# Attention decode backward on one core: where two more dK products stand relative to the softmax's reciprocal

## The chip, the cores and the metric

The kernel runs on one core of one Trainium2 chip. The metric is the device time of one execution in microseconds. Three executions of the kernel before took 634.61, 634.72 and 635.17 us; their median, 634.72 us, is the time before.

## The reference

There are 32 heads, each with one query row of 128 values and 8192 rows of K and of V, all in bf16. The reference returns the output and the three gradients of a softmax attention:

```
scores = einsum('bhqd,bhkd->bhqk', q, k) * 128 ** -0.5
p      = softmax(scores, axis=-1)
out    = einsum('bhqk,bhkd->bhqd', p, v)
# vjp with grad_out (the kernel's do):
dV = p outer do                 # 8192 x 128 per head
dp = V . do,  ds = p * (dp - sum(p * dp)) * scale
dK = ds outer q                 # 8192 x 128 per head
dq = ds . K
```

K and V are read once and dK and dV are written once: 134.23 MB each way by the profile. Each value read is used in very few operations.

## The kernel before, in words

The heads are worked in 16 pairs. In turn `t` of the main loop the pair `t` is "now" and the pair `o = t - 1` is "old". A pair's K is one SBUF tile of 128 partitions by 128 rows of 128 values, 4 MB; its V has the same shape. Three K tiles and two V tiles are used in rotation. The products dK and dV are written over K and V in place, and the stores read from these same tiles. That gives the cycle that every turn obeys: the tile is loaded, read by TensorE and VectorE, overwritten on VectorE by its gradient, stored, and, when the store has landed, loaded again for a later pair.

A pair passes through these steps, with the engine that does each:

- `k_block(t, c)`, eight of them: VectorE transposes an eighth of K (L197), TensorE multiplies it with q into the bank `s_ps` (L205).
- `s_back`, `s_top`, `s_exp`, `s_sum`: VectorE takes the scores back and their maximum (L212, L217, L219), TensorE turns the maximum (L220), VectorE makes the bias `nbias` (L227), ScalarE makes the exponentials `e` (L230), TensorE sums them over the partitions (L235, into `m_ps`).
- `p_of`: VectorE takes the reciprocal `rinv` of that sum (L246) and a scaled copy `p_s` (L251). ScalarE makes `p_rep` from `e` and `rinv` (L248) and puts it into the windows `win_p` (L241).
- `contract(t, "p")`: TensorE multiplies V with `win_p` (L341, `acc_p`), for the output.
- `v_bank`, `v_copy` and `v_scores`: TensorE transposes V (L269, `T_ps`), sixteen banks of four 128x128 pieces, ScalarE copies each bank out (L275, `XV_sb`), TensorE multiplies with `do` (L286, `dp_ps`). Three PSUM buffers serve the banks.
- `v_back`, `pd_sum`, `ds_of`, `contract(t, "ds")`: VectorE takes dp back (L312, `dpT`), and the softmax gradient `ds` is made and contracted with K.
- `outer(t, "p", r)` and `outer(o, "ds", r)`, eight of each: VectorE overwrites block `r` of V with dV, or of K with dK (both L363). A block of V can be overwritten only after `contract(t, "p")` and the transposes of that block have read it. `dk(a, b)` runs the dK products `a` to `b - 1` of the old pair, and issues the store (L373) that a finished part allows.

All instructions stand on each engine in the order in which the Python code lists them: no scheduler moves them, and each engine works through its own list in order. All loads and large stores are issued from one queue, SyncE's, in list order too.

There are two kinds of turn. In turns 3 to 14 (`wide(t)`, "with V blocks") half of V is transposed by VectorE instead of TensorE. Turns 0, 1, 2 and 15 do without V blocks, and all sixteen banks of V go over TensorE; turn 16 has only the dK products of the last pair and the small results. In turn 0 there is no old pair, so `dk` issues nothing.

In turns 1, 2 and 15 VectorE's order in the kernel before is: dK products 0 to 2, the scores' way back and `nbias`, dK product 3, the reciprocal, `p_s`, dK products 4 to 7, dV products 0 and 1, `v_back`, dV product 2, `ds`, and the other dV products. The dK store follows product 7 (in turn 15 there are two half stores, after products 3 and 7); the dV store follows dV product 7 (in turn 15 there are four, after every second product).

Of the kernel before, what the change touches and what calls it, by code (L numbers as in the profile page):

```python
# [15 lines left out]
NB = 8  # L16
# [11 lines left out]
def kernel(  # L28
# [54 lines left out]
    def load_k(t, parts=1):  # L83
        load(k, Kt, t, parts)
# [124 lines left out]
    def s_back(t):  # L209
        x = st[t]  # L210
        x["sT"] = backs.tile([P, BN, QD], F32, tag="back", name="sT")
        nc.vector.transpose(x["sT"][:].rearrange("p n r -> p (n r)"), x.pop("s")[:])  # L212

    def s_top(t):
        x = st[t]
        mx = small.tile([P, 1], F32, tag="mx")
        nc.vector.reduce_max(mx[:], x["sT"][:, :, 0:NB], axis=AX.XY)  # L217
        top = small.tile([P, 1], F32, tag="top")
        nc.vector.tensor_scalar_mul(top[:], mx[:], scale)  # L219
        nc.tensor.transpose(x["m"][:, 128:256], top[:].to_broadcast([P, P]), ident_f[:])  # L220

    def s_exp(t):
        x = st[t]
        nbias = small.tile([P, 1], F32, tag="nbias")
        for s in range(2):
            a, b = s * HF, (s + 1) * HF
            nc.vector.tensor_reduce(nbias[a:b], x["m"][a:b, 128 + a:128 + b], axis=AX.X, op=ALU.max, negate=True)  # L227
        e = x["e"] = single.tile([P, NT], F32, tag="e", name="e")
        rs = small.tile([P, 1], F32, tag="rs")
        nc.scalar.activation(e[:].rearrange("p (c n) -> p n c", c=NB), x["sT"][:, :, 0:NB], ACT.Exp, bias=nbias[:],  # L230
                             scale=scale, accum_out=rs[:])
        return rs
# [20 lines left out]
    def wide(t):  # L253
        return 3 <= t < HP - 1

    def v_bank(t, m):
        x = st[t]
        z, i = divmod(m, NM // TB)
        if t == 0:
            if i == 0:  # L260
                x["XV", z] = k_in[2][:].rearrange("p n d -> p (n d)").bitcast(F32).rearrange(
                    "p (z m s) -> p z m s", z=NZ, s=P)[:, z]
        elif i == 0:
            x["XV", z] = xvpool.tile([P, NM, P], F32, tag="XV", name="XV_sb")[:]
        T_ps = psT.tile([P, TB, P], F32, tag="T", name="T_ps")
        words = Vt[t][:].rearrange("p n d -> p (n d)").bitcast(F32)
        for j in range(TB):
            at = (i * TB + j) * NZ + z
            nc.tensor.transpose(T_ps[:, j, :], words[:, at * P:(at + 1) * P], ident_f[:])  # L269
        x["T", m] = T_ps  # L270

    def v_copy(t, m):
        x = st[t]
        z, i = divmod(m, NM // TB)
        nc.scalar.copy(x["XV", z][:, i * TB:(i + 1) * TB, :], x.pop(("T", m))[:])  # L275
# [14 lines left out]
    def v_block(t, r):  # L290

        X = xkpool.tile([P, NM, NW, QD], F32, tag="XK", name="XV_blk")
        nc.vector.transpose(X[:], Vt[t][:].rearrange("p n d -> p (n d)").bitcast(F32).rearrange(  # L293
            "p (m r w j) -> p m r w j", r=SL, w=NW, j=QD)[:, :, SL // 2 + r])
        st[t]["XW", r] = X
# [63 lines left out]
    def outer(t, which, r):  # L359
        x = st[t]  # L360
        X, row = (Kt[t], 0) if which == "ds" else (Vt[t], 1)
        a, b = r * BN, (r + 1) * BN
        nc.vector.tensor_tensor(  # L363
            X[:, a:b, :].rearrange("p n (a b) -> p n a b", b=R),
            x[which][:, a:b, :].unsqueeze(2).to_broadcast([P, BN, D // R, R]),
            x["qd"][:, row, :].rearrange("p (a b) -> p a b", b=R).unsqueeze(1).to_broadcast([P, BN, D // R, R]),
            op=ALU.mult)

    def store(t, which, parts=1, last=None):
        X, dst = (Kt[t], out_2) if which == "ds" else (Vt[t], out_3)  # L370
        L = NT // parts
        for c in (range(parts) if last is None else (last,)):
            nc.sync.dma_start(rows_of(dst, t, c * L, (c + 1) * L), X[:, c * L:(c + 1) * L, :])  # L373
# [15 lines left out]
    def v_part(t, m):  # L389
        v_bank(t, m)  # L390
        v_copy(t, m)
# [19 lines left out]
    for t in range(HP + 1):  # L411
        o = t - 1
        now, old = t < HP, t > 0
        parts = 4 if o == HP - 1 else 2 if o == HP - 2 else 1

        def dk(a, b):
            for r in range(a, b if old else a):
                outer(o, "ds", r)
                if (r + 1) % (NB // parts) == 0:
                    store(o, "ds", parts, r * parts // NB)  # L420

        blocks = now and wide(t)

        if blocks:

            dk(0, 5)
            s_back(t)
            s_top(t)
            for m in range(3):
                v_bank(t, m)  # L430
            v_block(t, 0)
            rs = s_exp(t)
            for m in range(3):
                v_copy(t, m)
            v_block(t, 1)
            v_part(t, 3)
            s_sum(t, rs)
            v_scores(t, 0)
            v_wide(t, 0)
            dk(5, 6)  # L440
            p_of(t)
            v_part(t, 4)
            v_part(t, 5)
            v_block(t, 2)
            v_wide(t, 1)
            v_part(t, 6)
            v_part(t, 7)
            v_block(t, 3)
            contract(t, "p")
            v_scores(t, 1)  # L450
            v_wide(t, 2)
            v_wide(t, 3)
            weights_do(t + 1)
            if wide(t + 1):
                weights_wide(t + 1)
        else:
            dk(0, 3)
            if now:
                if old:
                    v_part(t, 3)  # L460
                    v_part(t, 4)
                s_back(t)
                s_top(t)
                if old:
                    v_scores(t, 0)
                    v_part(t, 5)
                    v_part(t, 6)
                rs = s_exp(t)
                if old:
                    for m in (7, 8, 9):  # L470
                        v_bank(t, m)
                s_sum(t, rs)
                if old:
                    v_copy(t, 7)
                    v_copy(t, 8)
            dk(3, 4)
            if now:
                p_of(t)
                if old:
                    v_copy(t, 9)  # L480
                    v_scores(t, 1)
                    v_part(t, 10)
                    v_part(t, 11)
                contract(t, "p")
                if old:
                    v_part(t, 12)
                    v_part(t, 13)
                    v_scores(t, 2)
                    v_part(t, 14)
                    v_part(t, 15)  # L490
                    v_scores(t, 3)
                if t + 1 < HP:
                    if old:
                        weights_do(t + 1)
                    if wide(t + 1):
                        weights_wide(t + 1)
        if not now:
            dk(4, NB - 1)
            results()
            dk(NB - 1, NB)  # L500
            break
        dk(6 if blocks else 4, NB)
        fine = t == 0 or t == HP - 1
        outer(t, "p", 0)
        outer(t, "p", 1)
        if fine:
            store(t, "p", 4, 0)
        v_back(t)
        pd_sum(t)
        if t % ST == 0 and old:  # L510
            gather(o, "ds")
        outer(t, "p", 2)
        ds_of(t)
        contract(t, "ds")
        if t % ST == ST - 1:
            gather(t, "p")
        if t + 1 < HP:
            prepare(t + 1)
        else:
            gather(t, "ds")  # L520
        for r in range(3, NB):
            outer(t, "p", r)
            if fine and r % 2:
                store(t, "p", 4, r // 2)
            if t + 1 < HP and t != 1 and r >= HALF - 1:
                k_block(t + 1, r - HALF + 1)
        if not fine:
            store(t, "p")
        if t == 1:
            for c in range(HALF + 1):  # L530
                k_block(t + 1, c)
        if t + 1 < HP:
            for c in range(HALF + 1, NB):
                k_block(t + 1, c)
                if not wide(t + 1):
                    v_part(t + 1, c - HALF - 1)
            if t + 2 < HP:
                weights_q(t + 2)
        if 0 < t and t + 2 < HP:
            load_k(t + 2)  # L540
        if t + 2 < HP:
            load_v(t + 2, 4 if t == 0 else 1)
# [32 lines left out]
```

## Time and profile before

| what | value |
|---|---|
| median of three executions | 634.72 us (634.61 to 635.17) |
| the profiled execution's own time | 635.36 us |
| span in its profile, first to last instruction | 633.6 us |
| VectorE (DVE) busy | 558.9 us, 88% |
| TensorE (PE) busy | 428.7 us, 68% |
| ScalarE (ACT) busy | 158.0 us, 25% |
| the large DMA queue (q1) | 268.47 MB, 99.2% of 16 engines' span |
| DMA over the span | 424 GB/s |

The profiled execution took 1.76 us more than its span; this lies around the first and the last instruction. It is 0.64 us above the median, so a sum made on the span is taken to the median by its difference alone. "Busy" is the time of an engine's instructions, and a share of the span. In the timeline a row holds the start, the duration, the engine, the line of the kernel, the operation, what it writes and reads, and how many instructions are merged; in brackets stands how long the engine was idle ahead of the row, and what released it.

### The profile page before, as it was taken

To read this page: it belongs to the slowest core of one execution; us is meant where nothing else is said; L and a number is where in the kernel's file an instruction comes from. 1 tells how busy PE (TensorE), PEld (TensorE's weight loads), DVE (VectorE), ACT (ScalarE), POOL (GpSimd) and SP (SyncE) were. 2 spreads that over 40 slices of the span, in tenths; PEclk is the share of its full clock that TensorE was granted. 3 is DMA by queue.
4 is the path that set the end of the run, shared out by engine and by line. 5 is a ranking of instruction groups with operands and counts; after the bars stand their busy time and mean duration, and the time that the engine had idled before them with its cause. 6 is when DMAs were issued, how large, how long until landed. Compare 5 with 4: busy or idle time off the path is not lost.

```text
span 633.6 us, 7259 instructions
## 1 busy us (share of the span) xinstructions
PE 428.7 (68%) x2876; PEld 231.2 (36%) x2876; DVE 558.9 (88%) x662; ACT 158.0 (25%) x407; POOL 9.5 (1%) x27
## 2 busy tenths in 40 slices
PE   6767777766685765847766676765768658576860
PEld 5225335242341523315342332523425233152630
DVE  3788997999979899998998989899898899989793
ACT  6013416031230412204031130311303113040520
POOL 2000000000000000000000000000000000000000
PEclk9879888879789777798878798687986878887865
DMA  8999999999999999999999999999999999999997
GB/s 355 440 428 398 438 418 415 425 430 409 432 433 431 435 431 431 435 432 431 429 431 430 432 431 430 430 432 438 436 426 434 431 434 427 432 430 429 426 414 325
DMA packets 12177, 268.92 MB, mean 424 GB/s; under 512 B 1520, under 2 KB 1520, under 8 KB 1520
## 3 DMA queue, kind: packets, MB, share of 16 engines
q1 hardware_dynamic: 12096, 268.47, 99.2%
q8 instruction: 22, 0.36, 0.2%
q14 instruction: 11, 0.09, 0.0%
q10 hardware_dynamic: 48, 0.01, 0.0%
HBM read 134.23 MB, written 134.23 MB: 424 GB/s over the span
## 4 chain that ended last, share of the span: by engine, by line
DVE 38%; DMA 27%; PE 22%; issue 9%; ACT 2%; DVEq 0%; SPq 0%; ACTq 0%
DVE XK_sb L197 15%; DMA K<-in_k_dram 14%; DMA out_dram<-K 13%; DVE K L363 11%; PE T_ps L269 10%; DVE V L363 6%; PE dp_ps L303 5%; PE acc_p L341 3%; PE dp_ps L286 2%; ACT XV_sb L275 1%; DVE sT L212 1%; DVE dpT L312 1%; PE m_ps L220 1%; DMA V<-in_v_dram 1%; DVE ds_rep L331 1%
## 5 line engine op out<-in xcount | busy, mean ns | idle before, releaser
L205 PE MATMUL s_ps<-XK_sb,q_win 128*128 128x512 bf16 x512 | 148.6, 431 | 50.5 <-DVE XK_sb L197 48.3
L197 DVE STREAM_TRANSPOSE XK_sb<-K 128x1024 f32<-128x1024 f32 x128 | 152.2, 1221 | 3.5 <-DMA K<-in_k_dram 3.3
L363 DVE TENSOR_TENSOR V<-p_rep,qd 128x2048 bf16<-128x2048 bf16 x128 | 152.0, 1203 | 3.2 <-DMA K<-in_k_dram 2.0
L363 DVE TENSOR_TENSOR K<-ds_rep,qd 128x2048 bf16<-128x2048 bf16 x128 | 147.8, 1207 | 0.1
L269 PE MATMUL T_ps<-ident_f,V 128*128 128x128 f32 x640 | 108.1, 333 | 0.3 <-DMA V<-in_v_dram 0.2
L205 PEld LDWEIGHTS <-q_win 128*128 128x128 bf16 x512 | 53.4, 106 | 138.6 <-issue 102.7
L269 PEld LDWEIGHTS T_ps<-ident_f,V 128*128 128x128 f32 x640 | 97.5, 176 | 14.5 <-ACT XV_sb L275 1.6
L275 ACT COPY XV_sb<-T_ps 128x512 f32<-128x512 f32 x144 | 79.0, 586 | 78.7 <-PE T_ps L269 78.3
L293 DVE STREAM_TRANSPOSE XV_blk<-V 128x1024 f32<-128x1024 f32 x48 | 59.6, 1241 | 9.1 <-PE dp_ps L303 8.7
L341 PE MATMUL acc_ds<-K,win_ds 128*32 128x512 bf16 x512 | 47.8, 540 | 27.8 <-ACT win_ds L241 27.8
L220 PE MATMUL m_ps<-ident_f,top 128*128 128x128 f32 x16 | 6.2, 389 | 72.6 <-DVE top L219 72.6
L303 PE MATMUL dp_ps<-XV_blk,do_wide 128*128 128x512 bf16 x192 | 51.2, 399 | 0.0
L182 ACT COPY q_win<-q_blk 128x16 bf16<-128x16 bf16 x16 | 4.2, 260 | 156.7 <-PE s_ps L205 156.2
L341 PE MATMUL acc_p<-V,win_p 128*32 128x512 bf16 x512 | 32.1, 394 | 2.6 <-ACT win_p L241 2.4
L341 PEld LDWEIGHTS <-win_ds 128*32 128x32 bf16 x512 | 15.9, 122 | 48.1 <-ACT win_ds L241 27.2
L220 PEld LDWEIGHTS m_ps<-ident_f,top 128*128 128x128 f32 x16 | 2.6, 161 | 79.4 <-issue 71.4
L286 PE MATMUL dp_ps<-XV_sb,do_win 128*32 128x512 bf16 x288 | 24.3, 413 | 8.1 <-ACT XV_sb L275 8.1
L230 ACT ACTIVATE e<-sT,nbias 128x128 f32<-128x128 f32 x16 | 8.2, 515 | 80.8 <-DVE nbias L227 80.8
L303 PEld LDWEIGHTS <-do_wide 128*128 128x128 bf16 x192 | 17.3, 100 | 28.3 <-issue 14.3
L312 DVE STREAM_TRANSPOSE dpT<-dp_ps 128x512 f32<-128x512 f32 x16 | 11.5, 717 | 13.9 <-PE dp_ps L303 13.0
L341 PEld LDWEIGHTS <-win_p 128*32 128x32 bf16 x512 | 13.0, 99 | 16.3 <-issue 6.7
L321 PE MATMUL m_ps<-pd,same 128*128 128x1 f32 x32 | 6.1, 260 | 18.8 <-DVE m_ps L315 18.8
(68 smaller groups left out, 203.4 us busy)
## 6 DMA issues: line engine op xcount, KB each, us to landing
K<-in_k_dram SPq DMA_DIRECT2D x15, 4096.0 KB, 19.3
V<-in_v_dram SPq DMA_DIRECT2D x14, 4096.0 KB, 19.3
out_dram<-K SPq DMA_DIRECT2D x14, 4096.0 KB, 26.3
out_dram<-V SPq DMA_DIRECT2D x14, 4096.0 KB, 18.4
V<-in_v_dram SPq DMA_DIRECT2D x8, 1024.0 KB, 9.6
out_dram<-V SPq DMA_DIRECT2D x8, 1024.0 KB, 12.8
K<-in_k_dram SPq DMA_DIRECT2D x4, 1024.0 KB, 16.3
out_dram<-K SPq DMA_DIRECT2D x2, 2048.0 KB, 11.9
```

The source lines that it names most:

```text
L197: nc.vector.transpose(X[:], Kt[t][:, c * BN:(c + 1) * BN, :].rearrange("p n d -> p (n d)").bitcast(F32).rearrange("p (n w j) -> p n w j", ...
L205: nc.tensor.matmul(x["s"][:], lhsT=q_win[:, 2 * w + e2, SL - 1 - c:SL - 1 - c + P], rhs=cols[:, w, e2], start=(c == 0 and w == 0 and e2 == 0),
L220: nc.tensor.transpose(x["m"][:, 128:256], top[:].to_broadcast([P, P]), ident_f[:])
L230: nc.scalar.activation(e[:].rearrange("p (c n) -> p n c", c=NB), x["sT"][:, :, 0:NB], ACT.Exp, bias=nbias[:], scale=scale, accum_out=rs[:])
L269: nc.tensor.transpose(T_ps[:, j, :], words[:, at * P:(at + 1) * P], ident_f[:])
L275: nc.scalar.copy(x["XV", z][:, i * TB:(i + 1) * TB, :], x.pop(("T", m))[:])
L286: nc.tensor.matmul(x["dp"][b * QD:(b + 1) * QD, :], lhsT=do_win[:, b // 2, e2, at:at + QD], rhs=cols[:, e2, :, b * QD:(b + 1) * QD], start ...
L293: nc.vector.transpose(X[:], Vt[t][:].rearrange("p n d -> p (n d)").bitcast(F32).rearrange("p (m r w j) -> p m r w j", r=SL, w=NW, j=QD)[:, ...
L303: nc.tensor.matmul(st[t]["dp"][:], lhsT=do_wide[:, 2 * w + e2, at:at + P], rhs=cols[:, w, e2], start=False, stop=(r == SL // 2 - 1 and w = ...
L312: nc.vector.transpose(dpT[:].rearrange("p m r -> p (m r)"), x.pop("dp")[:])
L341: nc.tensor.matmul(acc[which][b * QD:(b + 1) * QD, :], lhsT=win[which][:, g, at:at + QD], rhs=X[:, 4 * g:4 * g + 4, :].rearrange("p n d -> ...
L363: nc.vector.tensor_tensor(X[:, a:b, :].rearrange("p n (a b) -> p n a b", b=R), x[which][:, a:b, :].unsqueeze(2).to_broadcast([P, BN, D // ...
```

## The change

In the turns without V blocks that have an old pair and a new one (1, 2 and 15), dK products 4 and 5 of the old pair are put ahead of `p_of`, so that six dK products stand ahead of the reciprocal instead of four. The loop that issues the rest then begins at 6 in these turns, as it did in the turns with V blocks. In turn 16 the two edits of `dk` ranges give the same products in the same order.

```
@@ -473,7 +473,7 @@
                 if old:
                     v_copy(t, 7)
                     v_copy(t, 8)
-            dk(3, 4)
+            dk(3, 6)
             if now:
                 p_of(t)
                 if old:
@@ -495,11 +495,11 @@
                     if wide(t + 1):
                         weights_wide(t + 1)
         if not now:
-            dk(4, NB - 1)
+            dk(6, NB - 1)
             results()
             dk(NB - 1, NB)
             break
-        dk(6 if blocks else 4, NB)
+        dk(6, NB)
         fine = t == 0 or t == HP - 1
         outer(t, "p", 0)
         outer(t, "p", 1)
```

The lists of ScalarE, TensorE, GpSimd and SyncE are the same in both kernels. On VectorE the reciprocal and `p_s` stand two products later in three places, and nothing else differs.

More of the change, by code (lines that the diff above doesn't have):

```diff
@@ L475 @@
                     v_copy(t, 8)
-            dk(3, 4)
+            dk(3, 6)
             if now:
@@ L497 @@
         if not now:
-            dk(4, NB - 1)
+            dk(6, NB - 1)
             results()
@@ L501 @@
             break
-        dk(6 if blocks else 4, NB)
+        dk(6, NB)
         fine = t == 0 or t == HP - 1
```

## Prediction

> **What bounds the kernel now.** I read the page first. VectorE is busy for 88% of the span and leads the chain of waits with 38%, so a VectorE stall looks like money. The DMA rows say otherwise:
>
> ```profile
> DMA  8999999999999999999999999999999999999997
> q1 hardware_dynamic: 12096, 268.47, 99.2%
> ```
>
> The first row is the mean busy share of the 16 DMA engines in 40 slices; only the ends are below 9. The second is the one large queue: 268.47 MB, with packets in flight for 99.2% of the 16 engines' span. Busy need not mean bound, so I looked at the order of landing in the stretch that the change touches (turn 1 runs from about 54 to 89 us). SyncE's timeline gives the issues:
>
> ```profile
> 68.95 0.34 SPq L373 DMA_DIRECT2D out_dram<-K  x1
> 80.30 0.34 SPq L373 DMA_DIRECT2D out_dram<-V  x1
> 84.58 0.34 SPq L81 DMA_DIRECT2D K<-in_k_dram  x1
> ```
>
> and the DMA view, in a window around each of these, gives size and time to landing (last column, us):
>
> ```profile
> out_dram<-K SPq DMA_DIRECT2D x1, 4096.0 KB, 15.6
> out_dram<-V SPq DMA_DIRECT2D x1, 4096.0 KB, 13.9
> K<-in_k_dram SPq DMA_DIRECT2D x1, 4096.0 KB, 19.4
> ```
>
> Issue plus time to landing: the dK store lands at 84.55, the dV store at 94.2, the K load at 104.0. They land in order of issue, 9.65 and 9.8 us apart, while each has been queued for longer than that. So the queue works in order and one 4 MB transfer takes 9.7 us of it; what a transfer needs beyond 9.7 us is time that it stood behind others. I call that its cover: 15.6 - 9.7 = 5.9 us for the dK store, 4.2 us for the dV store, 9.7 us for the K load. A transfer issued earlier only waits longer; one issued later costs nothing until its cover is used up. In turn 2 it is the same: dK store 20.0 us to landing, cover 10.3; dV store 13.8, cover 4.1. In turn 15 the two half dK stores take 13.5 and 10.4 us against 4.85 of their own, the 1 MB dV stores 8.7 against 2.4, and the very last dK store 9.1 against 2.4. The whole run is 64 such 4 MB transfers: 64 x 9.7 = 621 us of 633.6. The DMA queue is the bound.
>
> **What is stalled where.** VectorE's timeline of turn 1, with the idle time before a row in brackets:
>
> ```profile
> 59.88 1.23 DVE L363 TENSOR_TENSOR K<-ds_rep,qd 128x2048 bf16<-128x2048 bf16 x1
> 63.82 0.17 DVE L246 RECIPROCAL rinv<-m_ps 128x1 f32<-128x1 f32 x1 [2.72 <-PE m_ps L235]
> 64.30 4.62 DVE L363 TENSOR_TENSOR K<-ds_rep,qd 128x2048 bf16<-128x2048 bf16 x4
> 68.84 2.35 DVE L363 TENSOR_TENSOR V<-p_rep,qd 128x2048 bf16<-128x2048 bf16 x2
> 71.49 0.72 DVE L312 STREAM_TRANSPOSE dpT<-dp_ps 128x512 f32<-128x512 f32 x1 [0.30 <-PE dp_ps L286]
> ```
>
> VectorE stands idle for 2.72 us ahead of the reciprocal, in front of work (four dK products) that was ready. It is idle again, for only 0.30 us, ahead of `dpT`. That second bracket names TensorE, whose own timeline is:
>
> ```profile
> 59.76 3.80 PE L269 MATMUL T_ps<-ident_f,V 128*128 128x128 f32 x20
> 63.36 0.42 PE L235 MATMUL m_ps<-rs,same 128*128 128x1 f32 x2
> 65.60 1.91 PE L341 MATMUL acc_p<-V,win_p 128*32 128x512 bf16 x32
> 67.44 1.09 PE L269 MATMUL T_ps<-ident_f,V 128*128 128x128 f32 x8
> 70.83 0.62 PE L286 MATMUL dp_ps<-XV_sb,do_win 128*32 128x512 bf16 x8 [0.72 <-ACT XV_sb L275]
> ```
>
> The sum (L235) stands behind twenty transposes of V; the last dp matmuls end at 71.45, just before `dpT`. Turns 2 and 15 are alike: 2.83 us of idle time ahead of the reciprocal in both, and 0.31 and 0.36 us ahead of `dpT`.
>
> **The change, step by step.** (1) Two products go into the hole. Four in a row took 4.62 us, 1.155 each, so 2.31 us. Product 3 starts at 59.88; three of them end near 59.88 + 3.45 = 63.33 (3.45 is what three in a row took at 54.32). The reciprocal was released at 63.8, so it starts when it did, with 0.45 us to spare; in turn 15, 593.28 + 3.45 = 596.73 against 597.34, 0.6 to spare. Cost nothing; the cover is TensorE's twenty transposes. Behind the reciprocal stand `p_s` on VectorE, and `p_rep` with three bank copies queued after it on ScalarE; TensorE's `acc_p` and everything down to the last dp matmul wait for these. None of them moves. That the products themselves grow beside TensorE's transposes I put at nothing: the three at 54.32 ran beside such transposes and bank copies.
>
> (2) After `p_s` two dK products are left instead of four, so they end at 64.30 + 2.31 = 66.6 instead of 68.9, and the dK store is issued 2.3 us sooner. SyncE's list is unchanged and nothing stands between. The store lands at 84.55 as before, because the queue in front of it is what it waits for: its time to landing grows to 17.9. The K load that waits for this landing stays at 84.58. Gain nothing.
>
> (3) dV products 0 and 1 come next on VectorE, but they overwrite V, which TensorE still reads: `acc_p` until 67.5, and the transposes of these blocks in the first half of the row at 67.44, to about 68.0 (68.5 if the wait covers the whole row). So VectorE waits about 1.4 us here, where it did not wait before, and the two products end at about 70.4 (70.9).
>
> (4) `dpT` waits for TensorE at 71.45 as before; its idle time goes from 0.30 to about 1.1 us (0.6). The 2.31 us taken from the hole come back as 1.4 + 0.8 ahead of these two rows. From `dpT` on, VectorE stands where it stood, and so do the dV store and the next pair's scores.
>
> Sum per turn: 0; three turns: 0. The span stays 633.6 and the profiled time 635.36; from the median, 634.72 + 0 = 634.7 us.
>
> What the trace doesn't settle are two small ends. Below: the earlier second half store in turn 15 (602.46 to about 600.2) might fill a thin place, since between 600 and 604 the 16 engines' share dips to 0.62 to 0.85 for parts of a microsecond; the missing share there adds up to under 0.5 us, so at most 0.5 us is won. Above: if the two products overran the release by up to 0.5 us per turn, `dpT` and the dV store would be 0.5 us late against a cover of 4.1 us, so again nothing. I take 0 and keep -0.5 for the range.
>
> **Rivals.** *Faster: the DMA queue follows VectorE.* If DMA were only busy and not the bound, and if `dpT` could come earlier too, the 3 x 2.31 = 6.9 us would be won: 634.7 - 6.9 = 627.8 us. For it: VectorE's 88% and its lead in the chain. Against it: steps 2 to 4, two independent reasons, and the landings 9.65 to 9.8 us apart. It needs `dpT` in the profile after to start 2 us earlier. 0.08. The Trainium skill, Perfetto Trace Analysis, "Identifying the Most-Contended Engine", speaks for it: occupancy is called misleading for the 16 DMA engines, and bytes moved should be judged instead. Here the two agree by what the rows show, 424 GB/s over the span and the even landings; by the 435 GB/s ceiling that DMA: Bandwidth & Descriptors gives under "Specifications" the bytes would need 617 us, an estimate that leaves some 16 us of room.
>
> *Slower: TensorE's chain is granted less clock.* The granted clock is uneven in exactly this stretch (columns: window, its length, busy time of PE, PEld, DVE, ACT, POOL, then the clock, the DMA share and GB/s):
>
> ```profile
> 62.00:64.00 2.00, 2.00 (x14) 1.83 (x16) 0.17 (x1) 1.08 (x4) 0.00 (x0) 0.51 1.02 430
> 64.00:66.00 2.00, 1.86 (x24) 1.12 (x20) 1.91 (x3) 1.85 (x5) 0.00 (x0) 1.00 1.00 422
> ```
>
> If VectorE's new work beside the transposes went with a longer half-rate stretch, the chain from the sum to `dpT` (about 7.6 us of TensorE rows between 63.36 and 71.45) would stretch with it. A half-rate stretch like that from 60.5 to 64 costs some 1.7 us. The point from which it decides is the dV store's cover, 4.1 to 4.2 us: one or two stretches more cost nothing, three cost 5.1 - 4.2 = 0.9 us per turn. In turns 1 and 2 that is 1.8 us, 636.5 us; with the whole chain at half rate 7.6 - 4.2 = 3.4 us per turn, 641.5. Against it: TensorE's list and its idle gaps are untouched. 0.09. The Trainium skill, TensorE: Matmul & The Clock Gate, Part 1, makes the gate follow TensorE's own recent activity in a free-running window, so that its phase may vary between runs; by it the change has no handle on the clock, and the trace agrees in so far as the 0.51 follows TensorE's own wait at 57 to 59 us.
>
> *The change does nothing as written.* VectorE's list does differ in the three places, so that is excluded; what remains is that it does so to no effect, which is the forecast.
>
> **How the numbers follow.** Forecast, no change: 0.83. Faster by the rival: 0.08. Slower: 0.09. A measurement of this kernel can tell about 0.2% (1.27 us) from no change, and the forecast with its ends lies inside that, so the chances of faster, same and slower are 0.08, 0.83 and 0.09. The range is the forecast's own, which with 0.83 holds what is asked: the lowest execution less the 0.5 us end and 0.2 of scatter, 634.61 - 0.7 = 633.9, to the profiled execution's time plus 0.2, 635.6.
>
> **What would show it.** In the profile after, for turn 1: idle ahead of the reciprocal 0.4 to 0.5 us and its start still 63.8; the dK store issued near 66.6 with a time to landing of 17.9; new idle time of about 1.4 us ahead of dV product 0, about 1 us ahead of `dpT`, and `dpT` still at 71.5; dV store at 80.3 and K load at 84.6. The forecast is wrong if `dpT` starts over 0.5 us earlier and the landings move with it, or if landings in a row come more than 10 us apart because the dV store was issued after its cover had run out.

## The result, and the profile after

The changed kernel takes 636.76 us (median of 13, 635.51 to 637.04) against 635.11 us for the kernel before on the same chip (median of 13, 634.61 to 635.69). The ratio is 1.0022, with a 95% interval of 1.0015 to 1.0030: the kernel became slower by about 1.4 us by the ratio (the medians lie 1.65 us apart). Its 13 times form two groups: three lie at 635.5 to 635.9 and ten at 636.35 to 637.04. The profile after is of the shortest one, 635.51 us with a span of 633.7, beside 633.6 before. So the first profile shows where the two products went, but hardly the loss.

VectorE's timeline of turn 1 after, to be laid beside the rows of before:

```profile
59.90 3.50 DVE L363 TENSOR_TENSOR K<-ds_rep,qd 128x2048 bf16<-128x2048 bf16 x3
63.90 0.17 DVE L246 RECIPROCAL rinv<-m_ps 128x1 f32<-128x1 f32 x1 [0.51 <-PE m_ps L235]
64.38 2.35 DVE L363 TENSOR_TENSOR K<-ds_rep,qd 128x2048 bf16<-128x2048 bf16 x2
68.06 2.36 DVE L363 TENSOR_TENSOR V<-p_rep,qd 128x2048 bf16<-128x2048 bf16 x2 [1.33 <-ACT XV_sb L275]
71.61 0.72 DVE L312 STREAM_TRANSPOSE dpT<-dp_ps 128x512 f32<-128x512 f32 x1 [1.18 <-PE dp_ps L286]
```

This is the forecast, row for row: 0.51 us are left of the hole, the dV products wait 1.33 us, and `dpT` starts at 71.61 (71.49 before). The bracket of the dV products names ScalarE's copies, but the last of those in front of it ended at 67.1; the eight transposes of V on TensorE that began at 67.53 took 1.09 us, and their first half ends near 68.1, so the wait fits them, as step 3 said. SyncE's timeline and, in the second fence, the DMA view around each issue (last column: us to landing) after:

```profile
66.76 0.34 SPq L373 DMA_DIRECT2D out_dram<-K  x1
80.42 0.34 SPq L373 DMA_DIRECT2D out_dram<-V  x1
84.52 0.34 SPq L81 DMA_DIRECT2D K<-in_k_dram  x1
```

```profile
out_dram<-K SPq DMA_DIRECT2D x1, 4096.0 KB, 17.7
out_dram<-V SPq DMA_DIRECT2D x1, 4096.0 KB, 13.7
```

The dK store is issued 2.2 us sooner and still lands at 84.5; the dV store lands at 94.1. The queue's row is the same to the last digit as before:

```profile
q1 hardware_dynamic: 12096, 268.47, 99.2%
```

What belongs to this execution alone is on TensorE:

```profile
59.78 3.86 PE L269 MATMUL T_ps<-ident_f,V 128*128 128x128 f32 x20
63.44 0.43 PE L235 MATMUL m_ps<-rs,same 128*128 128x1 f32 x2
```

Twenty transposes in 3.86 us, as in the profile before (3.80). The granted clock in 60 to 64 us was 0.63 and 0.52. This is not how most of the traces of this case look: in 11 of 14 these twenty transposes of turn 1 take 2.5 us.

### The profile page after: what moved, and what is told of

It is laid out like the page before. It is cut to its first block, busy times and chain, and to the rows that moved or that the text cites. A ratio compares the mean times of both kernels' runs of the same rounds, so it can differ in the third digit from the quotient of the medians.

```text
span 633.7 us, 7259 instructions
## 1 busy us (share of the span) xinstructions
PE 427.7 (67%) x2876; PEld 229.6 (36%) x2876; DVE 559.3 (88%) x662; ACT 157.7 (25%) x407; POOL 9.5 (1%) x27
## 3 DMA queue, kind: packets, MB, share of 16 engines
HBM read 134.23 MB, written 134.23 MB: 424 GB/s over the span
## 4 chain that ended last, share of the span: by engine, by line
DVE 36%; DMA 31%; PE 19%; issue 9%; ACT 3%; DVEq 0%; SPq 0%; ACTq 0%
DMA out_dram<-K 18%; DVE XK_sb L197 15%; DMA K<-in_k_dram 12%; DVE K L363 11%; PE T_ps L269 10%; DVE V L363 5%; PE dp_ps L303 4%; PE acc_p L341 2%; PE dp_ps L286 2%; ACT XV_sb L275 1%; DVE sT L212 1%; DVE dpT L312 1%; DMA V<-in_v_dram 1%; PE m_ps L220 1%; ACT K L275 1%
## 5 line engine op out<-in xcount | busy, mean ns | idle before, releaser
L205 PE MATMUL s_ps<-XK_sb,q_win 128*128 128x512 bf16 x512 | 150.9, 433 | 52.1 <-DVE XK_sb L197 49.1
L269 PE MATMUL T_ps<-ident_f,V 128*128 128x128 f32 x640 | 106.2, 329 | 0.7 <-DMA V<-in_v_dram 0.4
L269 PEld LDWEIGHTS T_ps<-ident_f,V 128*128 128x128 f32 x640 | 95.8, 173 | 14.8 <-issue 1.9
L303 PEld LDWEIGHTS <-do_wide 128*128 128x128 bf16 x192 | 17.2, 100 | 27.8 <-issue 13.6
```

Of the source, the lines that this page charges most:

```text
L205: nc.tensor.matmul(x["s"][:], lhsT=q_win[:, 2 * w + e2, SL - 1 - c:SL - 1 - c + P], rhs=cols[:, w, e2], start=(c == 0 and w == 0 and e2 == 0),
L303: nc.tensor.matmul(st[t]["dp"][:], lhsT=do_wide[:, 2 * w + e2, at:at + P], rhs=cols[:, w, e2], start=False, stop=(r == SL // 2 - 1 and w = ...
```

## Experiments

All were timed in five rounds beside the kernel before on the same chip. Each has one profiled execution, which need not be a median one.

### Which turns, and is the loss real

**Six products ahead in turns 1 and 2 only** (the edit is to the kernel before).

```
-            dk(3, 4)
+            dk(3, 6 if t in (1, 2) else 4)
...
-        dk(6 if blocks else 4, NB)
+        dk(6 if blocks or t in (1, 2) else 4, NB)
```

> The change in turns 1 and 2 alone. Theory 'early': the loss comes from the first turns, where the two dK stores enter the DMA queue 2.2 us sooner; then this kernel is 1.0 to 1.8 us slower than before (ratio 1.0016 to 1.0028). Theory 'tail': the loss comes from turn 15, where the last stores are issued; then this kernel is within 0.4 us of before. Theory 'chance' (nothing real, the executions of both kernels only scatter): within 0.4 us, as are all four of this set.

Measured: 636.40 us (11 runs, 635.79 to 636.97) against 635.24; ratio 1.0017 (1.0008 to 1.0026).

**Six products ahead in turn 15 only** (`t == HP - 1` in the place of `t in (1, 2)`).

> The change in turn 15 alone. 'Tail': 1.0 to 1.8 us slower than before. 'Early': within 0.4 us. 'Chance': within 0.4 us. If both parts are slower by about half each, neither theory holds and the loss is a sum.

Measured: 635.13 us (11 runs, 634.79 to 635.49), ratio 0.9999 (0.9990 to 1.0008). Turn 15 costs nothing; the loss is that of turns 1 and 2. (In this trace the products overran the hole of turn 15 too: VectorE was not idle ahead of its reciprocal, which started at 597.61 us, 0.9 us after the sum.)

**The changed kernel again, and the kernel before against itself.**

> The changed kernel once more. 'Early' and 'tail': ratio 1.0015 to 1.003 as in the first comparison, most executions near 637.0 and a few near 635.6. 'Chance': ratio near 1.000. In its profile, if this execution is a long one, the extra 1.4 us should show as landings more than 9.7 us apart at one place: before 130 us by 'early', after 595 us by 'tail'.

> The kernel before, unchanged, as a measure of what the comparison itself can tell: ratio 1.000 within 0.0008 by every theory but 'chance', which expects it to scatter as the changed kernel does (634.6 to 637.0).

Measured: 636.67 us, ratio 1.0021 (1.0012 to 1.0030), and 635.40 us, ratio 1.0001 (0.9992 to 1.0010). The loss repeats, and a kernel against itself shows none. The profiled execution of the repeat took 637.13 us (span 635.3), so this is a trace of the long group. The expectation had its loss at one place; the landings show it in steps: against the trace of "turn 15 only", the V loads of turns 1, 2 and 3 land 0.4, 0.7 and 1.6 us later. Its VectorE timeline in turn 1:

```profile
60.62 3.50 DVE L363 TENSOR_TENSOR K<-ds_rep,qd 128x2048 bf16<-128x2048 bf16 x3
64.15 0.17 DVE L246 RECIPROCAL rinv<-m_ps 128x1 f32<-128x1 f32 x1
...
71.82 0.72 DVE L312 STREAM_TRANSPOSE dpT<-dp_ps 128x512 f32<-128x512 f32 x1 [1.16 <-PE dp_ps L286]
```

and its TensorE timeline:

```profile
60.51 2.48 PE L269 MATMUL T_ps<-ident_f,V 128*128 128x128 f32 x20
62.82 0.31 PE L235 MATMUL m_ps<-rs,same 128*128 128x1 f32 x2
```

The reciprocal has no bracket: VectorE was not idle ahead of it, it was still at the products. The transposes took 2.48 us and not 3.86, and the sum was ready 1 us before the reciprocal started. The "turn 15 only" kernel still has four products ahead in turn 1, and its profiled execution happens to reach product 3 at the same time, so it is the fair partner:

```profile
60.63 1.23 DVE L363 TENSOR_TENSOR K<-ds_rep,qd 128x2048 bf16<-128x2048 bf16 x1
63.17 0.17 DVE L246 RECIPROCAL rinv<-m_ps 128x1 f32<-128x1 f32 x1 [1.31 <-PE m_ps L235]
...
70.98 0.72 DVE L312 STREAM_TRANSPOSE dpT<-dp_ps 128x512 f32<-128x512 f32 x1 [0.44 <-PE dp_ps L286]
```

The hole is 1.31 us. Products of 2.31 us overrun it by 1.0: the reciprocal goes from 63.17 to 64.15, `dpT` from 70.98 to 71.82, the dV store from 79.78 to 80.63. Turn 2 of the repeat has an overrun of the same size. Over the five traces here with four products ahead in these turns (the two of the kernel before, this one, and two from further below), the hole of turn 1 is 2.72 us in the profile before and 1.31 in the other four; that of turn 2 is 2.83 in two and 1.31 or 1.32 in three. The length depends on the clock that this execution's transposes were granted. Clock windows (columns as in the prediction) of the repeat:

```profile
60.00:62.00 2.00, 2.00 (x22) 1.53 (x22) 1.82 (x4) 0.80 (x2) 0.00 (x0) 1.00 0.99 418
62.00:64.00 2.00, 1.94 (x21) 1.45 (x20) 2.00 (x2) 1.63 (x5) 0.00 (x0) 1.00 1.04 438
```

The granted clock is 1.00 here, where the profiles before and after had 0.64 and 0.51, and 0.63 and 0.52. The Trainium skill, TensorE: Matmul & The Clock Gate, Part 1, says that the gate's window runs freely and that its effect varies from run to run; the trace agrees, with 2.48 or 3.80 us for the same twenty transposes.

That explains 0.8 to 1 us of lateness per turn, but not yet a loss: the dV store of the repeat is issued at 80.63 and lands 13.6 us later, at 94.2, just as its partner's does (79.78 + 14.5 = 94.3).

### Is it the late dV store?

**Both dV stores of turns 1 and 2 in two halves**, the first one issued after dV product 3; all else as in the changed kernel.

```
+            if t in (1, 2) and r == HALF - 1:
+                store(t, "p", 2, 0)
...
-        if not fine:
+        if t in (1, 2):
+            store(t, "p", 2, 1)
+        elif not fine:
             store(t, "p")
```

> The changed kernel, with the dV stores of turns 1 and 2 issued as two halves, the first after dV product 3. Theory 'late dV': with six products ahead the reciprocal is often later than TensorE's sum, so the dV stores of turns 1 and 2 are issued 0.3 to 1.6 us later than before, just as the quickest DMA engines reach the end of the queue. The first half store is issued over 4 us sooner, so the loss should go: within 0.5 us of before, or faster than it. Theory 'early dK': the loss comes from the dK stores that enter the queue 2 us sooner; they still do here, so 1.0 to 1.8 us slower than before.

Measured: 637.05 us (6 runs), ratio 1.0026 (1.0015 to 1.0038). The loss stayed, which speaks against the late dV store as far as this one number goes. The trace shows a loss at another place, turn 3, where the whole store came back; SyncE's timeline, and the windows there:

```profile
159.94 0.34 SPq L373 DMA_DIRECT2D out_dram<-V  x1
```

```profile
158.00:162.00 4.00, 2.91 (x14) 1.16 (x13) 4.00 (x4) 0.00 (x0) 0.00 (x0) 1.00 0.69 295
188.00:192.00 4.00, 3.79 (x35) 1.35 (x36) 4.00 (x4) 0.20 (x2) 0.00 (x0) 0.57 1.04 360
```

At 158 to 162 the DMA share is 0.69: the queue ran dry. VectorE reached turn 3's reciprocal 2.4 us later than in the repeat of the kernel before (135.57 against 133.13), lost another 2.2 us inside turn 3 while TensorE's clock was halved (more on this below), and now met a store in one piece. So this run settled nothing by itself, and the next series repeats it further out.

**The kernel before with only the dV stores of turns 1 and 2 made late**, by repeating dV product 7 (the same values are written again).

```
+        if t in (1, 2):
+            outer(t, "p", 7)
         if not fine:
             store(t, "p")
```

> The kernel before, with dV product 7 made twice (the same values again) in turns 1 and 2, so that these two dV stores are issued 1.15 us later and the dK stores when they were. 'Late dV': 0.8 to 2 us slower than before, as the changed kernel is. 'Early dK': within 0.4 us of before.

Measured: 638.61 us (5 runs), ratio 1.0054 (1.0041 to 1.0066). Nothing moved ahead of the reciprocal, its idle time is 1.31 us, and the late dV store alone (81.04 us in turn 1) loses 0.54%, some 3.4 us, where 0.8 to 2 us were expected. To be late with the dV store is enough, with no dK store moved. The repeated product also makes VectorE late for all that comes behind it; the halves in turns 1 to 5, below, bear on that.

**The changed kernel with the dK store late again**: dK product 7 behind dV product 0.

```
-        dk(6, NB)
+        dk(6, NB if blocks or not old else NB - 1)
         fine = t == 0 or t == HP - 1
         outer(t, "p", 0)
+        if not blocks:
+            dk(NB - 1, NB)
```

> The changed kernel, with dK product 7 moved behind dV product 0 in turns 1, 2 and 15, into idle time, so that the dK stores are issued near 70.4 us in turn 1 (before 68.95, changed 66.8), while the reciprocal and the dV stores stand as in the changed kernel. 'Late dV': still 1.0 to 1.8 us slower than before. 'Early dK': within 0.4 us of before.

Measured: 637.14 us (5 runs), ratio 1.0032 (1.0020 to 1.0045). The dK store goes out at 70.72, later than before the change, and the loss stays: the earlier dK store is not its cause.

**Five products ahead.**

```
-            dk(3, 6)
+            dk(3, 5)
...
-        dk(6, NB)
+        dk(6 if blocks else 5, NB)
```

> Five dK products ahead of the reciprocal in turns 1, 2 and 15 instead of four or six. The shortest idle time ahead of the reciprocal seen so far with four is 1.31 us, one more product takes 1.16, so the reciprocal is not held up, and the dK stores are issued 1.15 us sooner than before. 'Late dV': within 0.4 us of before. 'Early dK': about half of the loss, 0.5 to 1.0 us.

Measured: 635.03 us (11 runs), ratio 1.0001 (0.9992 to 1.0010). One product of 1.155 us fits into 1.31, and the row shows what is left:

```profile
62.73 0.17 DVE L246 RECIPROCAL rinv<-m_ps 128x1 f32<-128x1 f32 x1 [0.18 <-PE m_ps L235]
```

### How close to its limit the queue is

**The changed kernel with the dV stores of turns 1 to 5 in halves** (as above, with `0 < t < 6` for `t in (1, 2)`).

> The changed kernel (six ahead), with the dV stores of turns 1 to 5 issued as two halves, the first after dV product 3. In the run with halves in turns 1 and 2 only, the stretched DMA packets of 90 to 152 us were gone, but the 16 engines ran dry for 0.8 us at 158 to 161, where turn 3's whole dV store was issued at 159.94, and the stretched packets came after that. Theory 'queue runs out': VectorE is 2 us behind after turns 1 and 2, and the loss is made only where a dV store comes as the quickest DMA engines run out; with halves up to turn 5 the loss goes, within 0.5 us of before. Rival 'the lag itself': the late VectorE costs the time whatever the stores do; then 1.0 to 1.8 us slower than before.

Measured: 635.33 us (11 runs, 635.03 to 635.70), ratio 1.0003 (0.9994 to 1.0012). The loss is gone, though VectorE still overruns in turn 2 (in turn 1 this execution left 0.61 us of the hole). At turn 3's reciprocal it is 1.4 us behind the trace of the next run (135.63 against 134.23), and the two spans are 633.8 and 633.4 us; with whole stores a lag of 0.9 us goes with 1.5 us of span (the traces with six ahead in turns 1 and 2 only and in turn 15 only). So it is not the lag alone that costs the time. The half stores move in packets of 16 KB instead of 32 KB; no run has the smaller packets without the earlier issue in the changed kernel, so that rival stays open.

**The kernel before with the same halves.**

> The kernel before (four ahead), with the same half stores in turns 1 to 5. 'Queue runs out': its profile still shows 2.0 us of stretched packets (mean of the 16 engines) at 90 to 152 us; these go, so 0.5 to 2 us faster than before. 'The lag itself': within 0.4 us of before.

Measured: 635.24 us (11 runs), ratio 1.0002 (0.9993 to 1.0011). The gain expected did not come: the halves mend a loss, and where there is none they do nothing. The 2.0 us that were to go stood in the first profile; between 84 and 160 us the repeat of the kernel before has 0.35.

**Five ahead, and halves in turns 1 to 14** (`0 < t < HP - 1`).

> Five ahead in turns 1, 2 and 15, and half dV stores in turns 1 to 14. 'Queue runs out': as the last or a little better, 0.5 to 2 us faster than before, if the nine more half stores cost nothing. 'The lag itself': within 0.4 us.

Measured: 635.58 us (11 runs), ratio 1.0008 (0.9999 to 1.0017); no gain either.

**Seven products ahead** (the edit is to the kernel before).

```
-            dk(3, 4)
+            dk(3, 7 if now else 4)
...
-        dk(6 if blocks else 4, NB)
+        dk(6 if blocks else 7, NB)
```

> Seven dK products ahead of the reciprocal in turns 1, 2 and 15, whole dV stores. Both theories: the reciprocal is held up by 4 x 1.16 less the time to the sum, 1.1 us more per turn than with six, so the loss grows to 2.5 to 4 us, much as with the dV product made twice (3.4 us). If it stays at 1.4 us, the hold-up is not the cause.

Measured: 638.35 us (5 runs), ratio 1.0050 (1.0037 to 1.0062). One product more costs nearly another 0.3% (1.0050 against 1.0022); the dV store of turn 1 is at 81.65:

```profile
65.14 0.17 DVE L246 RECIPROCAL rinv<-m_ps 128x1 f32<-128x1 f32 x1
```

**What the queue does.** A transfer is spread over the 16 DMA engines, and the trace has a completion event of each. The landing is that of the slowest. At 84 us the quickest engine is 2.65 us ahead of it in the repeat of the changed kernel (2.6 to 3.1 in the other traces): it has finished the dK store at about 81.8 and needs the dV store then. The table gives the issue of turn 1's dV store, how long before the quickest engine's end of the dK store that is (margin), and what the packets between 84 and 200 us took above their usual time, 1.21 us for 32 KB (stretch, a sum from the packet records, mean of the 16 engines). All in us; the rows belong to one profiled execution each.

| kernel | dV store | margin | stretch | span |
|---|---|---|---|---|
| before, again | 78.98 | 2.82 | 0.53 | 633.1 |
| five ahead | 79.31 | 2.43 | 0.83 | 633.0 |
| turn 15 only | 79.78 | 2.06 | 1.79 | 633.0 |
| before (first profile) | 80.30 | 1.52 | 2.40 | 633.6 |
| after (first profile) | 80.42 | 1.49 | 2.62 | 633.7 |
| turns 1 and 2 only | 80.60 | 1.30 | 2.99 | 634.5 |
| after, again | 80.63 | 1.31 | 3.99 | 635.3 |
| dK store late | 80.68 | 1.15 | 4.10 | 635.4 |
| dV store late | 81.04 | 0.68 | 3.67 | 636.3 |
| seven ahead | 81.65 | 0.12 | 3.32 | 635.8 |

In the last two the queue also ran dry before 200 us, 0.47 and 0.76 us on the mean of the engines; in the others 0.11 at most. The less margin, the more stretch, but for two rows in which turn 3 has a part (below). The span follows only once the stretch passes about 2.5: after 600 us the queue runs dry for 3.7 and 3.6 us in the first two rows and for 2.4 to 3.1 in the rest, so up to there what is not lost early is lost at the end. The two first profiles, with half clock in both, sit at the edge.

Over the whole run the account closes. Stretch (the large queue's packets of 8 KB and more from 9 us on, each against its part of 1.213 us per 32 KB) and time run dry come to 7.7 to 7.9 us in the first three rows, 9.98 in "after, again", 11.14 and 10.42 in the last two; the span less this sum lies between 625.1 and 625.4 us in all ten. What the kernels differ by was lost in the queue. The last two rows have 1.8 and 1.3 us of stretch between 200 and 560 us (0.8 to 1.1 in the others), which the table leaves out; so their spans are longer than the table's stretch says.

"Turns 1 and 2 only" and "after, again" have the same margin at turn 1, yet their spans are 0.8 us apart. Turn 3 differs. Its granted clock (third from the end), first in "turns 1 and 2 only", then in "after, again":

```profile
136.00:138.00 2.00, 1.84 (x16) 0.94 (x16) 1.62 (x3) 1.39 (x4) 0.00 (x0) 1.00 0.76 328
136.00:138.00 2.00, 1.54 (x11) 0.45 (x11) 1.61 (x3) 1.69 (x4) 0.00 (x0) 0.50 0.76 328
```

In the second TensorE stays at half clock until about 141 us. `dpT` comes 11.1 us after turn 3's reciprocal instead of 8.8, the dV store goes out at 160.50 instead of 157.89, and 1.17 us of stretch follow between 160 and 200 us, against 0.08. Three of the six traces with six products ahead in turns 1 and 2 look like this ("after, again", "dK store late", halves in turns 1 and 2), and none of the other eight, where `dpT` comes 8.8 to 9.1 us after the reciprocal. Whether the change brings it about or chance does, no run shows; in those three traces it is part of the loss.

The stretch is seen in windows by GB/s (last column) while the share beside it stays near 1. A window counts a packet where it starts, and one of 4 us holds three or four packets of an engine, so a single rate swings; the row for 84 to 200 us is the steadier one. The kernel before, again:

```profile
108.00:112.00 4.00, 4.00 (x37) 1.39 (x33) 4.00 (x4) 0.37 (x1) 0.00 (x0) 0.59 1.03 426
188.00:192.00 4.00, 2.21 (x10) 0.79 (x9) 4.00 (x4) 0.00 (x0) 0.00 (x0) 1.00 0.99 418
84.00:200.00 116.00, 83.01 (x573) 44.32 (x571) 108.86 (x125) 31.23 (x82) 0.94 (x3) 0.88 1.00 430
```

The changed kernel, again:

```profile
108.00:112.00 4.00, 1.81 (x18) 0.94 (x22) 3.93 (x8) 1.09 (x5) 0.00 (x0) 0.83 0.99 311
188.00:192.00 4.00, 3.18 (x32) 1.08 (x32) 3.97 (x6) 0.59 (x2) 0.00 (x0) 0.64 0.97 336
84.00:200.00 116.00, 82.28 (x562) 44.65 (x561) 105.17 (x123) 31.13 (x81) 0.93 (x3) 0.85 1.00 418
```

The changed kernel with halves in turns 1 to 5:

```profile
84.00:200.00 116.00, 84.61 (x571) 44.89 (x570) 107.60 (x124) 31.03 (x81) 0.93 (x3) 0.85 1.00 431
```

Over 84 to 200 us the share is 1.00 in all three, yet the repeat of the changed kernel moves 418 GB/s where the others move 430 and 431: 3% less for 116 us, some 3 us. In single windows of 4 us up to a quarter less is moved (311 against 426), in part because packets start in a neighbouring window (104 to 108 us has 475). In the kernel with halves the stretch is 0.6, a 16 KB packet counted against half of 1.21 us. The stretch comes about every 20 us, near 90, 110, 130, 150, 170 and 190, where the queue goes over from loads to stores or back. With less margin the quick engines lose their lead (2.45 us at turn 1's dV store in "before, again", 1.92 in "after, again", 1.14 with seven ahead), so that the 16 change over closer together. That this is why the packets stretch is argued, not shown: no run sets the lead by itself.

## Why the prediction was wrong

- **Step 1, the hole: wrong in size, and with it the cover.** It put 2.31 us against 2.72 and had 0.45 us to spare. The 2.72 came from one execution whose twenty transposes ran mostly at half clock. With four products ahead the hole of turn 1 is 1.31 us in four of five traces, and in the long trace the products overrun it by 1.0 us in turns 1 and 2. The work named as cover, the transposes, was the right one; its length was the term that failed. In an execution where the transposes took 3.86 us step 1 held (0.51 us left).
- **The bound "Above": wrong.** It foresaw an overrun of up to 0.5 us and priced it at nothing, by a cover of 4.1 us for the dV store. That cover was read off the landing. At the quickest engine 2.8, 2.1 and 1.5 us were left in three traces with four products ahead, and the less was left, the more the packets stretched (0.5, 1.8 and 2.4 us). The landing of the dV store itself did not move (94.2 us).
- **What bounds the kernel: right, but read off too few landings.** The queue is the bound. Yet 9.7 us apart holds only for some landings: in the same profile the V loads of turns 1 and 2 land 10.4 and 10.9 us after the transfer ahead of them. That the queue has a rate of its own, which no late transfer changes, was the step from there to a price of nothing, and it failed: 418 GB/s against 430.
- **Step 2: right.** The dK store went out 2.2 us sooner and landed at the same time. With its issue put back to 70.72 the loss stayed.
- **Step 3: right**, 1.33 us of wait ahead of the dV products for 1.4 forecast.
- **Step 4: right in its rows, wrong in what follows.** The idle time ahead of `dpT` is 1.18 us for 1.1 forecast; but `dpT` stands where it stood only when step 1 holds. From "turn 15 only" to "after, again" it is 0.84 us later.
- **Turn 15: right in the time, not in the mechanism.** With the change there alone the ratio is 0.9999. But the 0.6 us to spare were not there: in both the profile after and "turn 15 only" the twenty transposes took 2.48 us instead of 3.96, and the reciprocal came 0.9 us after the sum. That this cost nothing was not what step 1 had reasoned.
- **The slower rival** had TensorE's chain as the place and the dV store as the victim. In turns 1 and 2, which it named, it had the clock with the wrong sign: there the loss comes with full clock, which shortens the hole. In turn 3 of the three traces above its mechanism is seen, a longer half-clock stretch and a later dV store. Its 636.5 us lies near the measured 636.76, by luck: the chain that it had stretched in turns 1 and 2 keeps its length, 7.7 to 7.8 us from the reciprocal to `dpT`, in every trace. Its point of decision, 4.1 us, was the same misread cover. That the gate's phase varies from run to run stood beside it, and was used to say that the change has no handle on the clock; it should have been turned on the 2.72 us.
- **The faster rival** fell: `dpT` did not come earlier in either profile of the changed kernel.
- **The starting point.** Of the 2.1 us between 634.7 and 636.76, 0.4 is the time before itself: 634.72 in three executions, 635.11 in thirteen.
- The forecast's own test, landings in a row more than 10 us apart, could not tell: the kernel before has such landings in the profile that the forecast was made from. The landings of turn 1's two stores were unchanged; the V loads of turns 1 to 3 and the GB/s of later windows showed the loss.

## What to carry to other kernels

Before work is moved into an idle time, measure that idle time in several executions and fill the shortest, above all when its length is set by matmuls whose granted clock changes from run to run: here 1.31 us was to be had, and one product fitted where two did not. Measure the slack of a transfer in a DMA queue at the quickest of its engines, and not by what its landing leaves: here 1.5 to 2.8 us and not 4.1. A queue that is busy all the time can still lose rate, so compare GB/s over windows of many packets and not the busy share.

## What was not expected of the hardware

The 16 engines of one queue drift apart: 2.65 us at 84 us in "after, again", 5.1 us at 604 us. The Trainium skill, DMA: Bandwidth & Descriptors, "Queues, rings and completion order", has a copy split over up to 16 rings, each with a tail pointer of its own; the trace agrees in that the parts of one copy end apart, and puts the number to it. Packets of other queues may make part of the lag (22 of 16 KB in one of them, about 1.0 us each), but no run shows it. And 32 KB packets, 1.21 us as a rule, took up to 2.7 us at the changes between loads and stores in the long execution (up to 2.08 in "before, again"), at a DMA share of 1.00 over 84 to 200 us.
